# A fused attention and mixer kernel: first attention with less weight conversion, first products beside the conversion, and a written order of instructions on TensorE

## The chip, the cores and the metric

The kernel runs on one core of one Trainium2 chip. The metric is the device time of one execution in microseconds (us), given as the median of several runs. A profiled run also has a span, from the first to the last instruction; it is 1.7 to 1.9 us shorter than the time of the same run.

## The reference

Four batches, eight heads, 768 positions, head width 48. A gated linear attention comes first; its output is a batch's x of 768 x 384, and a mixer with a low-rank step over the positions and two products with 384 x 1536 weights follows.

```python
f = 1.0 / (1.0 + np.exp(-f_logit))
for t in range(S):
    state = f[:, :, t, :, None] * state + np.einsum('bhd,bhe->bhde', k[:, :, t], v[:, :, t])
    y[:, :, t] = np.einsum('bhd,bhde->bhe', q[:, :, t], state)
# x = y as (B, S, H*D)
h = x.transpose(0, 2, 1) @ U @ V
u = x + h.transpose(0, 2, 1)
out = u + np.maximum(u @ w_ch1, 0.0) @ w_ch2
```

q, k, v, f_logit are float32. The four weights arrive as float64, and the kernel has to convert them itself.

## The kernel before

A **unit** is two heads of one batch: 16 units, four to a batch. A unit's attention goes through ten pieces: gates (transpose f on TensorE, sigmoid), kept keys (transposes of kT, copy to kb), keep (the scan X on VectorE), keys (kT), states (products ds, the scan st), scores (products sc, masked into A), read-back (the scan Y), read-out (products y from st), queries (qT) and inner products (y from A). The mixer has a low rank (ph), mixing (pu and an addition), a turn (put), 18 **first products** (pz, evicted to z by ScalarE with the Relu) and six **second products** (po) for batch 0; later batches use seven half-size products per pair (pw). The products of one batch are written between the attention pieces of the next as **fill**.

Each 64-bit weight slab costs two ScalarE, three VectorE and one GpSimd instruction:

```python
nc.scalar.activation(f, hi.bitcast(F32), AF.Abs)
nc.scalar.activation(r, lo, AF.Copy, scale=2.0**-29)
nc.vector.tensor_scalar(f, f, SMALLEST, LARGEST, ALU.max, ALU.min)
nc.vector.tensor_scalar(y, y, 3, 0x3FFFFFFF, ALU.logical_shift_left, ALU.bitwise_and)
nc.vector.scalar_tensor_tensor(y, hi, 0xC0000000, y, ALU.bitwise_and, ALU.bitwise_or)
nc.gpsimd.tensor_tensor(flat.bitcast(I32), y.bitcast(I32), r, ALU.add)
```

The second product of batch 0, one accumulation group of 12 matmuls (24 instructions in the trace):

```python
def ch2(a, s):
    t = 2 * a + s
    pm = ps_mm.tile([P, 512], F32, name="po", tag="mm")
    for i in range(NFC):
        nc.tensor.matmul(pm[:, 0:DM], lhsT=z[a, i // NI][:, i % NI, s * P : (s + 1) * P],
                         rhs=w2[:, i, :], start=(i == 0), stop=(i == NFC - 1))
    o = three.tile([P, DM], F32, name="o")
    nc.vector.tensor_tensor(o, x[:, t, :], pm[:, 0:DM], ALU.add)
    store(t, o)
```

The main loop (cut). A scheduler decides each engine's order; the recorded order is its hint.

```python
early = first - 7                     # eight weight slabs as fill of batch 0's attention
todo = [(1, f) for f in loads[:early]]
...
for b in range(B):
    fill = Fill(todo, HP * 10)
    for n in range(b * HP, (b + 1) * HP):
        kept, states, scores, read, inner = attend(n)
        gates, keep, keys, read_back, queries = prepare(n + 1)
        for piece in [gates, kept, keep, keys, states, scores, read_back, read, queries, inner]:
            fill()
            piece()
    fill.rest()
    m = mixer(b)
    if b == 0:
        start = NFC // 2 + NFC // 4   # nine first products beside the conversion
        for i, (_, piece) in enumerate(m.before + m.main[0:start]):
            if loads and (i % 2 == 0 or i >= len(m.before)):
                loads.pop(0)()
            piece()
        ...
        todo = m.main[start:]         # nine first and four second products fill batch 1
```

## Time and profile before

| | before |
|---|---|
| time, median | 575.3 us (575.49 in the runs beside the changed kernel) |
| TensorE busy, of the span of 573.6 us | 518.0 us, 90% |
| mean granted TensorE clock | 0.970 of full |

The table of stretches of the kernel before follows: start and end in us, length, then busy us and number of instructions of TensorE (PE), its weight loads, VectorE (DVE), ScalarE (ACT) and GpSimd (POOL), and the granted clock, the transfer engines' share and GB/s.

```profile
core 0: us, PE busy (x) PEld busy (x) DVE busy (x) ACT busy (x) POOL busy (x), PEclk, DMA share, GB/s
...
27.50:69.90 42.40, 28.22 (x659) 24.77 (x660) 36.07 (x49) 17.37 (x38) 6.98 (x7) 0.76 1.04 197
...
124.20:230.30 106.10, 97.63 (x998) 68.71 (x996) 54.90 (x57) 23.29 (x49) 7.25 (x4) 0.97 0.39 97
230.30:573.60 343.30, 328.94 (x3055) 290.35 (x3053) 143.96 (x190) 67.99 (x131) 22.79 (x12) 0.99 0.13 35
```

Read the length against PE busy: what is missing is idle time. In the rest of batch 0's attention (first row) TensorE works 28.2 of 42.4 us at a clock of 0.76, VectorE 36.1. In batch 1's attention (second row) TensorE is idle for 8.5 us, 8.4 of them in one wait of ds for kb, and the clock is nearly full. The last row, batches 2 and 3 and the end, has little left to win.

### The profile page before, as it was taken

To read this page: it belongs to the slowest core of one execution; us is meant where nothing else is said; L and a number is where in the kernel's file an instruction comes from. 1 tells how busy PE (TensorE), PEld (TensorE's weight loads), DVE (VectorE), ACT (ScalarE), POOL (GpSimd) and SP (SyncE) were. 2 spreads that over 40 slices of the span, in tenths; PEclk is the share of its full clock that TensorE was granted. 3 is DMA by queue.
4 is the path that set the end of the run, shared out by engine and by line. 5 is a ranking of instruction groups with operands and counts; after the bars stand their busy time and mean duration, and the time that the engine had idled before them with its cause. 6 is when DMAs were issued, how large, how long until landed. Compare 5 with 4: busy or idle time off the path is not lost.

```text
span 573.6 us, 12007 instructions
## 1 busy us (share of the span) xinstructions
PE 518.0 (90%) x5277; PEld 430.7 (75%) x5277; DVE 294.8 (51%) x390; ACT 146.0 (25%) x293; POOL 61.0 (11%) x63
## 2 busy tenths in 40 slices
PE   5676699799997699998999979998999999999996
PEld 4565568558864565888889867888889977898996
DVE  4788777964357753185766553186343141212132
ACT  3344356512221311222222112222121102201110
POOL 3011113420002110020211200020200000000000
PEclk9887799999999799999999989999999999999999
DMA  9599734716233525131533220010000000000000
GB/s 161 128 232 196 160 108 147 211 28 136 65 85 74 137 53 137 24 103 43 139 75 92 80 62 29 1 22 1 29 2 3 29 1 30 1 0 29 0 29 33
DMA packets 75307, 41.76 MB, mean 73 GB/s; under 512 B 65774, under 2 KB 68846, under 8 KB 75246
## 3 DMA queue, kind: packets, MB, share of 16 engines
q1 hardware_dynamic: 75246, 40.91, 30.6%
q8 instruction: 43, 0.70, 0.5%
q14 instruction: 18, 0.15, 0.1%
HBM read 36.18 MB, written 4.72 MB: 71 GB/s over the span
## 4 chain that ended last, share of the span: by engine, by line
PE 71%; DVE 18%; DMA 3%; ACT 3%; issue 2%; SPq 1%; POOL 1%; DVEq 0%; POOLq 0%; ACTq 0%
PE pz L157 26%; PE pw L194 22%; PE po L171 6%; PE y L590 3%; DVE X L465 3%; DMA f_raw<-in_f_logit_dram 3%; PE pt L433 3%; DVE w_y L62 3%; PE y L572 3%; PE pu L138 2%; PE ds L543 2%; DVE Y L482 2%; DVE fT L414 2%; PE sc L513 2%; PE put L147 2%
## 5 line engine op out<-in xcount | busy, mean ns | idle before, releaser
L157 PE MATMUL pz<-uT,w 128*128 128x256 f32 x864 | 196.4, 384 | 2.9 <-ACT z L162 2.3
L157 PEld LDWEIGHTS pz<-uT,w 128*128 128x128 f32 x864 | 162.2, 191 | 27.5 <-ACT z L162 3.7
L194 PE MATMUL pw<-w,w_raw 128*128 128x192 f32 x432 | 76.6, 333 | 4.1 <-DVE o L210 4.1
L162 ACT ACTIVATE z<-pz 128x512 f32<-128x512 f32 x72 | 42.7, 595 | 135.1 <-PE pz L157 131.0
L194 PEld LDWEIGHTS pw<-w,w_raw 128*128 128x128 f32 x432 | 71.7, 193 | 5.6 <-DVE o L210 4.9
L194 PE MATMUL pw<-w,z 128*128 128x192 f32 x324 | 56.5, 329 | 3.8 <-ACT z L162 3.8
L194 PEld LDWEIGHTS pw<-w,z 128*128 128x128 f32 x324 | 52.7, 190 | 5.5 <-ACT z L162 4.1
L171 PE MATMUL po<-w,z 128*128 128x384 f32 x144 | 48.7, 492 | 2.8 <-ACT z L162 1.8
L171 PEld LDWEIGHTS po<-w,z 128*128 128x128 f32 x144 | 26.6, 190 | 22.0 <-issue 2.8
L557 DVE TENSOR_TENSOR_SCAN st<-added,whole 128x576 f32<-128x576 f32 x16 | 21.6, 1352 | 37.3 <-ACT added L549 37.3
L465 DVE TENSOR_TENSOR_SCAN X<-fz,ends 128x768 f32<-128x768 f32 x16 | 29.8, 1863 | 21.1 <-ACT fz L454 13.6
L448 POOL TENSOR_TENSOR kT<-kT,X 128x768 f32<-128x768 f32 x8 | 14.6, 1821 | 238.2 <-DVE kT L414 179.9
L185 DVE TENSOR_TENSOR w_raw<-z 128x768 f32<-128x768 f32 x9 | 8.8, 978 | 56.6 <-ACT z L162 56.6
L572 PE MATMUL y<-st,qT 48*64 48x48 f32 x704 | 20.5, 268 | 14.0 <-DVE st L557 14.0
L590 PEld LDWEIGHTS y<-v_nat,A 64*64 64x64 f32 x768 | 26.4, 148 | 7.1 <-ACT seen L579 3.3
L64 POOL TENSOR_TENSOR w<-w_y,w_r 128x384 int32<-128x384 int32 x24 | 23.9, 995 | 66.8 <-DVE w_y L63 66.8
L590 PE MATMUL y<-v_nat,A 64*64 64x48 f32 x768 | 28.4, 232 | 2.8 <-ACT seen L579 2.8
L572 PEld LDWEIGHTS y<-st,qT 48*64 48x64 f32 x704 | 17.6, 157 | 17.4 <-issue 16.2
L482 DVE TENSOR_TENSOR_SCAN Y<-fz,starts 128x768 f32<-128x768 f32 x16 | 29.4, 1838 | 0.5
L543 PEld LDWEIGHTS ds<-v_nat,kb 64*64 64x64 f32 x768 | 15.6, 145 | 16.9 <-ACT kb L535 11.3
L543 PE MATMUL ds<-v_nat,kb 64*64 64x48 f32 x768 | 19.4, 233 | 9.1 <-ACT kb L535 9.0
L414 DVE STREAM_TRANSPOSE fT<-f_raw 128x768 f32<-128x768 f32 x8 | 16.7, 2086 | 9.9 <-POOL qT L448 7.9
(87 smaller groups left out, 491.2 us busy)
## 6 DMA issues: line engine op xcount, KB each, us to landing
w_raw<-in_moe_w_ch_dram SPq DMA_DIRECT2D x24, 384.0 KB, 3.7
v_nat<-in_v_dram SPq DMA_DIRECT2D x32, 144.0 KB, 3.5
out_dram<-o SPq DMA_DIRECT2D x24, 192.0 KB, 2.2
f_raw<-in_f_logit_dram SPq DMA_DIRECT2D x31, 142.0 KB, 3.6
k_raw<-in_k_dram SPq DMA_DIRECT2D x31, 142.0 KB, 2.9
q_raw<-in_q_dram SPq DMA_DIRECT2D x31, 142.0 KB, 3.8
f_raw<-in_f_logit_dram SPq DMA_DIRECT2D x16, 144.0 KB, 5.4
k_raw<-in_k_dram SPq DMA_DIRECT2D x16, 144.0 KB, 4.5
```

Of the source, the lines that this page charges most:

```text
L64: nc.gpsimd.tensor_tensor(flat.bitcast(I32), y.bitcast(I32), r, ALU.add)
L157: nc.tensor.matmul(pm[:, i * 2 * P : (i + 1) * 2 * P], lhsT=w1[:, m, o : o + P], rhs=uT[a][:, m, :], start=(m == 0), stop=(m == NDC - 1))
L162: nc.scalar.activation(z[a, c][:, k : k + 2, :].rearrange("p i t -> p (i t)"), pm, AF.Relu)
L171: nc.tensor.matmul(pm[:, 0:DM], lhsT=z[a, i // NI][:, i % NI, s * P : (s + 1) * P], rhs=w2[:, i, :], start=(i == 0), stop=(i == NFC - 1))
L194: nc.tensor.matmul(pm[:, n * HM : (n + 1) * HM], lhsT=lhs[:, i, :], rhs=rhs[:, i, :], start=(i == 0), stop=(i == NI - 1))
L414: nc.vector.transpose(t.rearrange("p (i c) -> p c i", c=TB), bass.AP(src_tile.tensor, src_tile.offset, [list(src_tile.ap[0]), [D, TB], [1, ...
L465: nc.vector.tensor_tensor_scan(backwards(X, S - 1, S), backwards(f, S, S), backwards(ends, S - 1, S), 0.0, ALU.mult, ALU.add,)
L482: nc.vector.tensor_tensor_scan(Y, f[:, 0:S], starts, 0.0, ALU.mult, ALU.add)
L543: nc.tensor.matmul(ds[par * PAD : (par + 1) * PAD, s, c * D : (c + 1) * D], lhsT=T["kb"][part[s], par, c, :], rhs=vt[part[s], c, par, :], ...
L557: nc.vector.tensor_tensor_scan(st, added[:, 0 : D * NCH], whole.rearrange("p e c -> p (e c)"), 0.0, ALU.add, ALU.mult)
L572: nc.tensor.matmul(o(c % 2, par, c // 2), lhsT=T["q"][rows[par], chunk[c]], rhs=T["st"][rows[par], c, :], start=(c <= 2), stop=False, skip ...
L590: nc.tensor.matmul(o(s, par, c), lhsT=T["A"][part[s], par, c, :], rhs=vt[part[s], c, par, :], start=False, stop=True, skip_group_check=True,)
```

## The change

Its intent: TensorE should not idle through the start. Batch 0's attention keeps only three weight slabs. All 18 first products of batch 0 run beside the rest of the conversion, so that only its six second products are left for batch 1. TensorE's order is the written one for the whole program, VectorE's up to batch 1. The operands of batches 2 and 3 are loaded in rows of 32 and 16 elements instead of rows that overlap. The change has further parts: the mixer's additions get a high priority in the scheduler's order, w1 is converted in slabs of 128 columns that reach over all three of its chunks, some buffers are no longer shared, and in batches 2 and 3 the kept keys come before the gates. The diff, cut to its core:

```diff
+        def add(*args):
+            with tc.high_priority(offset=AHEAD):
+                nc.vector.tensor_tensor(*args)
...
-            nc.vector.tensor_tensor(o, x[:, t, :], pm[:, 0:DM], ALU.add)
+            add(o, x[:, t, :], pm[:, 0:DM], ALU.add)
...
+        self.firsts = [p for j in range(NI) for a in range(NA) for p in [first(a)[j]]]
+        self.seconds = [p for a in range(NA) for p in second(a)]
...
-                    nc.sync.dma_start(
-                        out=dst[p0 : p0 + rows, :],
-                        in_=bass.AP(head.tensor, head.offset + part * NB, [[TB * D, rows], [1, W]]),
-                    )
+                    nc.sync.dma_start(
+                        out=raw[n % 2][nm][p0 : p0 + NB, :].rearrange("p (c d) -> p c d", d=NB)[:, :, 0:n_ch],
+                        in_=head[:, :, part * NB : part * NB + n_ch],
+                    )
...
+    ctx.enter_context(tc.manual_schedule(engines={nc.tensor.engine}))
+    with tc.manual_schedule(engines={nc.vector.engine}):
+        ready = {n: prepare(n) for n in range(2)}
+        for piece in ready[0] + ready[1][:1]:
+            piece()
+        for n in range(HP):
+            kept, states, scores, read, inner = attend(n)
+            _, keep, keys, read_back, queries = ready.pop(n + 1, [lambda: None] * 5)
+            if n + 2 < HP:
+                ready[n + 2] = prepare(n + 2)
+            gates = ready[n + 2][0] if n + 2 < HP else lambda: None
+            for piece in [kept, keep, keys, states, scores, read_back, gates, read, queries, inner]:
+                piece()
+            if n and loads:
+                loads.pop(0)()
+        m = mixer(0)
+        for i, (_, piece) in enumerate(m.before + m.firsts):
+            if loads and (i % 3 == 0 or i >= len(m.before)):
+                loads.pop(0)()
+            piece()
+        for f in loads:
+            f()
+        todo, after = m.seconds[:4], m.seconds[4:]
+        for i, piece in enumerate(prepare(HP)):
+            piece()
+            if i == 0:
+                todo.pop(0)[1]()
+        attention(1, todo)
+        m = start_mixer(1, after)
```

More of the change, by code (lines that the diff above doesn't have):

```diff
@@ L21 @@
 PAD = 64
+AHEAD = 1000
 LEAST = 1e-18
@@ L42, in load, with shaped @@
         rows, n = dst.shape[0], dst.free_size()
-        flat = dst if len(dst.shape) == 2 else dst.rearrange("p c n -> p (c n)")
         T = {}
+        def shaped(t):
+            return t if len(dst.shape) == 2 else t.rearrange("p (c n) -> p c n", c=dst.shape[1])
         def start():
             raw = T["raw"] = pool.tile([P, WP], U64, name="w_raw", bufs=RAW)[0:rows, 0:n]
-            if len(dst.shape) == 3:
-                raw = raw.rearrange("p (c n) -> p c n", c=dst.shape[1])
-            dma.dma_start(out=raw, in_=w)
+            dma.dma_start(out=shaped(raw), in_=w)
         def end():
@@ L63, in end @@
             nc.vector.scalar_tensor_tensor(y, hi, 0xC0000000, y, ALU.bitwise_and, ALU.bitwise_or)
-            nc.gpsimd.tensor_tensor(flat.bitcast(I32), y.bitcast(I32), r, ALU.add)
+            nc.gpsimd.tensor_tensor(dst.bitcast(I32), shaped(y.bitcast(I32)), shaped(r), ALU.add)
         return start, end
@@ L109, with __init__ @@
 class Mixer:
-    def __init__(self, nc, b, x, U, V, w1, w2, sums, ident, out, two, three, zp, ps_mm):
+    def __init__(self, tc, b, x, U, V, w1, w2, sums, ident, out, two, three, zp, ps_mm, wide=False):
+        nc = tc.nc
         P = nc.NUM_PARTITIONS
@@ L138, in mix @@
             nc.tensor.matmul(pm[:, 0:DM], lhsT=V[:, t * P : (t + 1) * P], rhs=h[0], start=True, stop=True)
-            nc.vector.tensor_tensor(x[:, t, :], x[:, t, :], pm[:, 0:DM], ALU.add)
+            add(x[:, t, :], x[:, t, :], pm[:, 0:DM], ALU.add)
         def turn(t):
@@ L160, in ch1 @@
             if k == 0:
-                z[a, c] = zp.tile([P, NI, 2 * P], F32, name="z")
+                own = wide and 2 * a + c >= 3
+                z[a, c] = zp.tile([P, NI, 2 * P], F32, name="zw" if own else "z")
             nc.scalar.activation(z[a, c][:, k : k + 2, :].rearrange("p i t -> p (i t)"), pm, AF.Relu)
@@ L183, in sums_of @@
                 S[i] = s.bitcast(F32).rearrange("p (i t) -> p i t", t=P)
-            add = nc.vector.tensor_tensor
             add(S[1], part(a, 1, 0), part(a, 1, 1), ALU.add)
@@ L202, in seven @@
             x0, x1 = x[:, 2 * a, :], x[:, 2 * a + 1, :]
-            add = nc.vector.tensor_tensor
             if step == 0:
@@ L260, in quarters, with place @@
     q = {(i, j): w2[:, i * NI : (i + 1) * NI, j * HM : (j + 1) * HM] for i in range(2) for j in range(2)}
-    sums = {i: pool.tile([P, NI, HM], F32, name=f"w2_{i}") for i in range(1, 4)}
-    sums[4] = q[0, 1]
+    sums = {4: q[0, 1]}
     sub = nc.vector.tensor_tensor
+    def place():
+        for i in range(1, 4):
+            t = pool.tile([P, NI, 2 * P], F32, name="zw")
+            sums[i] = t.rearrange("p i t -> p (i t)")[:, 0 : NI * HM].rearrange("p (i d) -> p i d", d=HM)
     return sums, [
+        place,
         lambda: sub(sums[1], q[0, 1], q[0, 0], ALU.subtract),
@@ L293, in factored_path @@
     TB = S // NB
-    W = (TB - 1) * D + NB
+    W = TB * NB
     G = NCH // 2
     TURNED = 2
-    assert S % (2 * P) == 0 and H % 2 == 0 and NB < D <= PAD and PAD == 2 * NB and S % NB == 0
+    assert S % (2 * P) == 0 and H % 2 == 0 and NB < D <= PAD and PAD == 2 * NB and S % NB == 0 and W == NBL * 2 * PAD
     assert DM % P == 0 and FF % P == 0 and FF % WP == 0 and DM == WP and DM <= 512 and R % 32 == 0 and P % R == 0 and P // R <= NBL and NFC % 4 == 0
@@ L314, in factored_path @@
     nat = [
-        {nm: t[:, 0 : NBL * 2 * PAD].rearrange("p (c h d) -> p c h d", h=2, d=PAD) for nm, t in slot.items()}
+        {nm: t.rearrange("p (c h d) -> p c h d", h=2, d=PAD) for nm, t in slot.items()}
         for slot in raw
@@ L334, in load_unit @@
                 continue
-            dst = raw[n % 2][nm]
             for par in range(2):
-                head = src[nm][b, 2 * hp + par]
+                head = src[nm][b, 2 * hp + par].rearrange("(i c) d -> i c d", c=TB)
                 for part in range(2):
                     p0 = par * PAD + part * NB
-                    last = n == NU - 1 and par == 1 and part == 1
-                    rows = NB - 1 if last else NB
+                    n_ch = min(NB, D - part * NB)
                     nc.sync.dma_start(
-                        out=dst[p0 : p0 + rows, :],
-                        in_=bass.AP(head.tensor, head.offset + part * NB, [[TB * D, rows], [1, W]]),
-                    )
-                    if last:
-                        w = W - (2 * NB - D)
-                        nc.sync.dma_start(
-                            out=dst[p0 + rows : p0 + NB, 0:w],
-                            in_=bass.AP(head.tensor, head.offset + part * NB + rows * TB * D,
-                                        [[TB * D, 1], [1, w]]),
-                        )
+                        out=raw[n % 2][nm][p0 : p0 + NB, :].rearrange("p (c d) -> p c d", d=NB)[:, :, 0:n_ch],
+                        in_=head[:, :, part * NB : part * NB + n_ch],
+                    )
         v_tiles[n] = three.tile([P, NBL, 2, D], F32, name="v_nat")
@@ L397, in factored_path @@
     weights += [load(V[:, o : o + WP], copies(moe_V, P // R, o, WP)) for o in range(0, S, WP)]
-    weights += [
-        load(w1[:, c, o : o + WP], moe_w_ch1[c * P : (c + 1) * P, o : o + WP])
-        for o in range(0, FF, WP)
-        for c in range(NDC)
-    ]
-    first = len(weights)
-    sums, to_sum = quarters(nc, const, w2)
+    w1_rows = moe_w_ch1.rearrange("(c p) f -> p c f", p=P)
+    weights += [load(w1[:, :, o : o + P], w1_rows[:, :, o : o + P]) for o in range(0, FF, P)]
+    sums, to_sum = quarters(nc, zp, w2)
     weights += [load(w2[:, i, :], moe_w_ch2[i * P : (i + 1) * P, :]) for i in range(NFC)]
@@ L415, in turned @@
             t.rearrange("p (i c) -> p c i", c=TB),
-            bass.AP(src_tile.tensor, src_tile.offset, [list(src_tile.ap[0]), [D, TB], [1, NB]]),
+            src_tile.rearrange("p (c d) -> p c d", d=NB),
         )
@@ L456, in gates @@
                 return
-            fT = one.tile([P, S], F32, name="fT", tag="Y")
+            fT = one.tile([P, S], F32, name="fT")
             turned(fT, r["f"])
@@ L480, in read @@
         def read():
-            Y = T["Y"] = one.tile([P, S], F32, name="Y", tag="Y")
+            Y = T["Y"] = one.tile([P, S], F32, name="Y")
             nc.vector.tensor_tensor_scan(Y, f[:, 0:S], starts, 0.0, ALU.mult, ALU.add)
@@ L493, in mixer @@
     def mixer(b):
-        return Mixer(nc, b, x_tiles[b], U, V, w1, w2, sums if b else None, ident, out, two, three, zp, ps_mm)
+        return Mixer(tc, b, x_tiles[b], U, V, w1, w2, sums if b else None, ident, out, two, three, zp, ps_mm, b == 0)
     def attend(n):
@@ L605, in factored_path, with attention @@
     loads = ahead_by(RAW - 1, weights)
-    early = first - 7
-    todo = [(1, f) for f in loads[:early]]
-    loads = loads[early:]
-    for piece in prepare(0):
-        piece()
-    after = []
-    for b in range(B):
+    def attention(b, todo):
         fill = Fill(todo, HP * 10)
@@ L619, in factored_path @@
                 order = [gates, kept, keep, keys, states, scores, read_back, read, queries, inner]
+                if (n + 1) // HP >= TURNED:
+                    order[0:2] = [kept, gates]
             else:
@@ L625, in factored_path, with start_mixer @@
         fill.rest()
+    def start_mixer(b, after):
         m = mixer(b)
-        if b == 0:
-            start = NFC // 2 + NFC // 4
-            for i, (_, piece) in enumerate(m.before + m.main[0:start]):
-                if loads and (i % 2 == 0 or i >= len(m.before)):
-                    loads.pop(0)()
-                piece()
-            for f in loads:
-                f()
-            todo = m.main[start:]
-            for i, f in enumerate(to_sum[:3]):
-                todo.insert(len(todo) - 4 + 2 * i, (1, f))
-        else:
-            after[1:1] = m.before[0:1]
-            after[3:3] = m.before[1 : 1 + NBL]
-            after += m.before[1 + NBL :]
-            if b == 1:
-                after.append((1, to_sum[3]))
-            for _, piece in after:
-                piece()
-            todo = m.main
@@ L648, in factored_path @@
-        after = m.after
+        pieces = after[:1] + m.before[:1] + after[1:2] + m.before[1 : 1 + NBL] + after[2:] + m.before[1 + NBL :]
+        for _, piece in pieces:
+            piece()
+        return m
+    ctx.enter_context(tc.manual_schedule(engines={nc.tensor.engine}))
[10 more added lines that the diff above has]
+            for piece in [kept, keep, keys, states, scores, read_back, gates, read, queries, inner]:
+                piece()
+            if n and loads:
[14 more added lines that the diff above has]
+        m = start_mixer(1, after)
+        for f in to_sum:
+            f()
@@ L650, in factored_path @@
+    for b in range(2, B):
+        todo, after = m.main, m.after
+        attention(b, todo)
+        m = start_mixer(b, after)
+    todo, after = m.main, m.after
     low = one.tile([P, 1], F32, name="low")
@@ L907, in mixer @@
     def mixer(b):
-        return Mixer(nc, b, x_tiles[b], U, V, w1, w2, None, ident, out, two, three, zp, ps_mm)
+        return Mixer(tc, b, x_tiles[b], U, V, w1, w2, None, ident, out, two, three, zp, ps_mm)
     FILLS = NL + 3
```

## The prediction

> **What bounds the kernel now.** I began with the busy rows in 40 slices of 14.3 us (tenths; the clock row is the granted TensorE clock).
>
> ```profile
> PE   5676699799997699998999979998999999999996
> DVE  4788777964357753185766553186343141212132
> PEclk9887799999999799999999989999999999999999
> ```
>
> The run has two regimes. Up to about slice 8 (124 us) TensorE is at 5 to 7 tenths, on a clock of 7 to 8 tenths in slices 1 to 4, and VectorE is the fuller engine. Later TensorE is nearly full. Next I read the chain that ended last, in order of time (start, duration, what).
>
> ```profile
> 15.15 12.29 DMA f_raw<-in_f_logit_dram
> 27.57 1.53 PE pt L433 x6
> ...
> 43.42 2.32 DVE X L465
> 46.03 0.87 DVE kT L445
> 47.07 1.76 DVE Y L482
> 48.82 1.26 DVE st L557
> 50.22 1.52 PE y L572 x44
> 51.74 1.47 PE pt L433 x6
> 53.21 2.19 PE y L590 x48
> 55.40 0.82 PE pt L433 x6
> ...
> 94.12 1.06 DVE w_y L62
> 96.07 1.06 DVE w_y L62
> ```
>
> Three things limit the start: a load for unit 2 that lands only at 27.5 us; a serial chain of 13.6 us per attention unit (42.59 to 56.24 from one gate to the next), with slow matmuls (1.47 us for six transposes that take 0.82 us warm); and the weight conversion, one slab per 1.95 us from 92 to 120 us. The costs come from the groups by form (busy us, mean ns):
>
> ```profile
> L157 PE MATMUL pz<-uT,w 128*128 128x256 f32 x864 | 196.4, 384 | 2.9 <-ACT z L162 2.3 <-ACT uT L149 0.4 <-POOL w L64 0.2
> L62 DVE TENSOR_SCALAR w_y<-w_y 128x384 uint32<-128x384 uint32 x26 | 21.1, 810 | 0.8
> L63 DVE SCALAR_TENSOR_TENSOR w_y<-w_raw,w_y 128x384 uint32<-128x384 uint32 x26 | 15.1, 582 | 0.7
> L64 POOL TENSOR_TENSOR w<-w_y,w_r 128x384 int32<-128x384 int32 x24 | 23.9, 995 | 66.8 <-DVE w_y L63 66.8
> ```
>
> Finally the waits of TensorE from 124 us to the end: what is left to win there.
>
> ```profile
> PE ds L543 <- ACT kb L535: 8.4, 1, 8.4
> PE pw L194 <- DVE o L210: 4.1, 1, 4.1
> PE pw L194 <- ACT z L162: 3.8, 2, 1.9
> ```
>
> **What the Trainium skill says.** "SBUF — State Buffer", section "SBUF: two separate sides", calls the port pair of VectorE and GpSimd an exclusive lock. The trace agrees: the shift (L62) takes 0.35 us alone and 1.05 us when a GpSimd add (0.99 us) runs; 0.35 + 1.05 + 0.55 is the 1.95 us. "TensorE: Matmul & The Clock Gate", Part 1, has a cold clock of half speed, released after some 3.4 us of activity; the 1.47 against 0.82 us above agrees. "PSUM — Partial Sum Buffer", "Engine vs sequencer instructions", says the ScalarE and VectorE queues are strict FIFO and matmuls keep their order; so the static orders of the changed program decide who waits behind whom. "DMA: Bandwidth & Descriptors", "Specifications", puts line rate at 512 B or more; here the 192-byte-row loads still moved 1.18 MB in about 7 us per unit when the queue was full.
>
> **The change part by part.** TensorE's arithmetic is unchanged, so I follow two clocks, where TensorE is free and where the in-order VectorE is.
>
> (1) Attention of batch 0. Conversion drops from eight slabs to three (U and two of V), and the next gates are issued one unit ahead. But unit 2's load stands in the same place of the same load queue, behind the V loads, so it again lands at 27.5 us; and now its transposes stand ahead of unit 0's read-out in TensorE's written order, so unit 0 waits too. From there: transposes to 29.1, read-out 1.2, query transposes 1.5, inner products 2.2, and unit 0 ends at 33.5 instead of 25.7. After that VectorE sets the pace: X 1.76 + small 0.56 + kT 0.95 + st 1.35 + A 0.95 + Y 1.76 + qT 0.95 = 8.3 us per unit, plus a slab. Scan X of unit 2 starts at 32.6, that of unit 3 at 41.9, unit 3's queries end at 50.2, V slab to 52, then kept keys, ds, st, read-out, inner, copy (0.8 + 0.9 + 0.65 + 1.3 + 1.2 + 2.2 + 0.6): low rank starts at **60 us, before 69.9**. Gain 10 us.
>
> (2) Low rank, mix, turn. On VectorE the x additions stand between slabs, so mixing waits: additions at 63.6 (2), one slab, 66.7 (3), one slab, 70.2 (1). First products start at **74.5, before 84**; the stage takes 14.5 us for 9.3 us of TensorE work (1.4 + 4.85 + 3.0).
>
> (3) All 18 first products, 12 matmul instructions each, 2.59 us apiece (23.58 us for 108): 46.6 us if TensorE were free. But ScalarE's compiled order puts two slabs (2 x 1.95 = 3.9 us) between one eviction and the next for the first nine. Slab 5 of w1/w2 ends about 76.7 on VectorE; the first eviction is at 78.8, the ninth at 78.8 + 8 x 3.9 = 110; with two PSUM buffers eight products are left: **done at 110.5 + 8 x 2.6 = 131.3**. The conversion ends near 112 (before 120.4), so this is 8 us earlier, but 10 us of TensorE time lie idle beside it, before 5.
>
> (4) Batch 1 attention. Before, nine first products and four second ones filled it; now only the six second ones (7.94 us each) remain, and VectorE follows the written order. Unit 4's X scan stands behind the addition of the first second product: 131.3 + 0.8 + 7.9 + 0.6 = 140.7. I followed the chain unit by unit. TensorE idles about 4 us in unit 4 (kT, then qT), 2.5 in unit 5, 2.5 in unit 6 (each waits for st), 4.6 in unit 7 (st stands behind an addition, kT and fT, 2.1 us each), and 3 in the mixing (a transpose and a scan stand between the x additions): 17 us. TensorE work: six times 7.94 = 47.6, attention 30, low rank to turn 9.3, together 87. So batch 1's first products begin at 131.3 + 87 + 17 = 235. In the kernel before they begin at 230.3, with 1.4 us of unit 8 already done: **behind by 6 us**. The gain of (1) is spent.
>
> (5) Batches 2 and 3. TensorE's sequence hardly differs. The 8.4 us wait (kb behind the gate of unit 8) lay before 230 and is gone, counted in (4). Of the 8 us of waits after 231, high-priority additions should take 4 to 5. The loads without double reading move a third less but in rows of 128 and 64 bytes: 12 x 768 + 1536 rows per unit. At the measured 0.8 us per 768-row load of a full queue that is, as an estimate, 11 us per unit against 23 us of unit time: hidden. The transpose is still 2.08 us.
>
> Sum: 573.6 + 6 - 5 = 574.6 us of span; the time is 1.7 us more (575.3 against 573.6): 576.3. I take **574**, since the hand chain takes each handover at its worst.
>
> **The rivals.** *The intended gain arrives:* conversion hides under first products at one slab per 2.6 us, attention 0 runs at 8.5 us per unit from 13 us on. It would end near 131 - 20 and give 550 to 558. For it: VectorE needs only 1.95 us of each 2.6 us. Against it: the 27.5 us landing and the two-slab order on ScalarE, both fixed by the build. *VectorE's written order becomes the bound in batch 1* more strongly than I count, with TensorE cold after each gap (0.6 us per group): 583 to 587. For it: the 1.47 us groups above. *The small-row loads become the wait* in batches 2 and 3: if such a row cost twice a 192-byte one, 22 us per unit would touch the 23 us available, and 5 to 10 us would be added. Against it: the load share there is 0 to 3 tenths.
>
> **Range and chances.** The chain up to 131 us I hold good to 4 us, batch 1 to 5, the rest to 4: together about 8 us, a little wider towards faster, where the first rival lies: **561 to 585**. Faster by over 2% means under 563.8 us: 0.15. Slower means over 586.8 us: 0.06. Within 2%: 0.79.
>
> **What would show it.** Step 1: TensorE's first wait still ends with unit 2's f load at 27 to 28 us; ph starts near 60. Step 2: pz starts near 74 to 75. Step 3: the first nine z are 3.9 us apart, the last pz ends near 131. Step 4: waits of y on st and of pt on kT or qT between 132 and 235, in sum some 14 us, and the batch 1 pz start at 233 to 238. Step 5: no DMA among TensorE's or VectorE's waits after 240. The prediction is wrong if f of unit 2 lands early, if evictions come every 2.6 us, or if batch 1's fill covers the chain; then the time falls below 563.

## The result, and the profile after

The changed kernel takes **593.85 us** (592.15 to 596.04, four runs) against 575.49 us (575.16 to 577.47): ratio **1.031**, interval 1.027 to 1.036. It is slower, and outside the predicted range. Executions over 1.5% slower than the fastest of the same kernel are left out of the means. A ratio is the mean time of one kernel's fast runs over that of the other's fast runs of the same rounds, so not quite the ratio of the medians quoted. The profiled run of the changed kernel, from which all its lines and stretches below come, is the slowest of the four (596.04 us). The changed kernel was not run again beside the later experiments, so differences from it of about 1% rest on ratios from different rounds.

The busy rows and the clock row of the changed kernel, in slices of 14.9 us, tenths:

```profile
PE   5396886799889869799979997999999999999996
DVE  4466399910762675749647576047531151122132
PEclk9786599999798678999999999999999999999998
```

The clock row has two troughs (slices counted from 0): slices 1 to 4, attention of batch 0, deeper than before; and a new one in slices 10 to 15, 149 to 238 us, attention of batch 1, where the row of before has nines and a single seven. The stretches, in the columns of the table above:

```profile
28.50:67.80 39.30, 31.50 (x734) 28.14 (x735) 24.07 (x33) 12.44 (x27) 4.88 (x4) 0.67 0.86 151
67.80:82.70 14.90, 12.46 (x42) 5.59 (x42) 8.28 (x17) 6.33 (x15) 2.92 (x3) 0.73 0.35 98
82.70:140.30 57.60, 48.77 (x217) 40.46 (x218) 36.59 (x59) 28.34 (x56) 20.00 (x21) 1.00 0.41 117
140.30:252.20 111.90, 97.59 (x1060) 65.66 (x1058) 64.71 (x71) 22.84 (x50) 8.42 (x4) 0.86 0.45 70
252.20:594.20 342.00, 327.15 (x3089) 288.58 (x3089) 146.62 (x194) 69.29 (x132) 22.80 (x12) 1.00 0.14 27
```

The fourth row is the finding: the stretch of batch 1's attention holds 15.4 us less of the mixer's products of batch 0 than before (six second products of 7.94 us instead of 5 x 7.94 + 9 x 2.59) and some 4 us more of the attention, since before part of unit 4 lay ahead of the stretch. Yet TensorE is busy just as long, 97.6 us, at a clock of 0.86, and is idle for 14.3 us instead of 8.5. It ends 22 us later than in the kernel before. How this looks in TensorE's order of time (start, length, what, in brackets the idle time just before it and what ended it; batch 0 first, then the first products, then batch 1):

```profile
28.55 1.51 PE L436 MATMUL pt<-ident,f_raw 128*128 128x128 f32 x6 [10.39 <-DMA f_raw<-in_f_logit_dram]
...
64.19 2.80 PE L593 MATMUL y<-v_nat,A 64*64 64x48 f32 x48 [0.25 <-ACT seen L582]
67.82 2.77 PE L135 MATMUL ph<-x,U 128*32 128x384 f32 x12 [0.83 <-ACT x L599]
...
91.80 2.83 PE L166 MATMUL pz<-uT,w 128*128 128x256 f32 x12 [1.05 <-ACT z L173]
96.04 2.86 PE L166 MATMUL pz<-uT,w 128*128 128x256 f32 x12 [1.42 <-ACT zw L173]
```

```profile
152.51 0.58 PE L534 MATMUL pt<-ident,kT 64*128 64x64 f32 x12 [1.71 <-DVE kT L448]
...
156.72 10.16 PE L182 MATMUL po<-w,z 128*128 128x384 f32 x24
...
168.78 1.60 PE L593 MATMUL y<-v_nat,A 64*64 64x48 f32 x48
...
173.58 0.89 PE L516 MATMUL sc<-qT,kT 48*64 48x64 f32 x48
176.59 1.23 PE L575 MATMUL y<-st,qT 48*64 48x48 f32 x44 [2.12 <-DVE st L560]
177.75 1.20 PE L436 MATMUL pt<-ident,q_raw 128*128 128x128 f32 x6
178.88 2.80 PE L593 MATMUL y<-v_nat,A 64*64 64x48 f32 x48
...
217.71 1.52 PE L575 MATMUL y<-st,qT 48*64 48x48 f32 x44 [4.37 <-DVE st L560]
219.48 2.80 PE L593 MATMUL y<-v_nat,A 64*64 64x48 f32 x48 [0.25 <-ACT seen L582]
222.20 9.85 PE L182 MATMUL po<-w,zw 128*128 128x384 f32 x24
```

The same 48 inner products take 1.60 us in one unit and 2.80 us in the next; the slow ones come after a wait for st. A whole second product, 7.9 us at full clock, takes 10.2 and 9.9 us. In the kernel before, first products stood between sc and y:

```profile
142.42 0.89 PE L513 MATMUL sc<-qT,kT 48*64 48x64 f32 x48
143.25 2.86 PE L157 MATMUL pz<-uT,w 128*128 128x256 f32 x12
146.03 1.24 PE L572 MATMUL y<-st,qT 48*64 48x48 f32 x44
```

The waits of TensorE and of VectorE in the changed kernel from 140 to 253 us (in total, times, longest):

```profile
PE y L575 <- DVE st L560: 8.6, 3, 4.4
```

```profile
DVE o L143 <- PE po L182: 60.4, 6, 28.2
```

Each engine waits for the other. VectorE stands before the addition of a second product until its 24th instruction is done (28.2 us of the 60.4 lie before the first of them, the other five waits come to 32.2), and what is written behind the addition, scans among it, is late; then TensorE stands before the read-out.

### The profile page after: what moved, and what is told of

Same layout as the page of the kernel before. It is cut to its first block, busy times and chain, and to the rows that moved or that the text cites. A ratio compares the mean times of both kernels' runs of the same rounds, so it can differ in the third digit from the quotient of the medians.

```text
span 594.2 us, 11997 instructions
## 1 busy us (share of the span) xinstructions
PE 528.4 (89%) x5277; PEld 437.3 (74%) x5277; DVE 293.8 (49%) x390; ACT 147.2 (25%) x293; POOL 63.5 (11%) x63
## 4 chain that ended last, share of the span: by engine, by line
PE 71%; DVE 18%; DMA 3%; ACT 3%; issue 2%; POOL 2%; SPq 1%; DVEq 0%; POOLq 0%; ACTq 0%
PE pz L166 26%; PE pw L204 19%; PE po L182 9%; PE y L593 5%; DVE w_y L65 3%; DMA f_raw<-in_f_logit_dram 3%; PE y L575 3%; PE pt L436 2%; DVE w_y L66 2%; PE ds L546 2%; DVE st L560 2%; PE pu L147 1%; DVE X L468 1%; DVE fT L417 1%; DVE w_y L64 1%
## 5 line engine op out<-in xcount | busy, mean ns | idle before, releaser
L173 ACT ACTIVATE z<-pz 128x512 f32<-128x512 f32 x63 | 37.5, 595 | 117.6 <-PE pz L166 113.4
L204 PE MATMUL pw<-zw,w_raw 128*128 128x192 f32 x324 | 56.2, 328 | 2.2 <-DVE o L143 2.2
L204 PEld LDWEIGHTS pw<-zw,w_raw 128*128 128x128 f32 x324 | 52.8, 190 | 3.7 <-DVE o L143 3.5
L143 DVE TENSOR_TENSOR w_raw<-z 128x768 f32<-128x768 f32 x18 | 20.4, 1132 | 57.3 <-ACT z L173 57.2
L593 PEld LDWEIGHTS y<-v_nat,A 64*64 64x64 f32 x768 | 30.3, 166 | 7.2 <-ACT seen L582 4.8
L593 PE MATMUL y<-v_nat,A 64*64 64x48 f32 x768 | 32.4, 250 | 3.0 <-ACT seen L582 3.0
L143 DVE TENSOR_TENSOR o<-x,po 128x384 f32<-128x384 f32 x6 | 3.3, 555 | 60.4 <-PE po L182 60.4
L575 PEld LDWEIGHTS y<-st,qT 48*64 48x64 f32 x704 | 18.4, 169 | 15.4 <-issue 12.1
L182 PE MATMUL po<-w,z 128*128 128x384 f32 x72 | 28.0, 549 | 0.0
L182 PE MATMUL po<-w,zw 128*128 128x384 f32 x72 | 25.9, 517 | 0.0
L147 PE MATMUL pu<-h,V 128*128 128x384 f32 x48 | 21.1, 561 | 4.3 <-DVE x L143 3.0
L65 DVE TENSOR_SCALAR w_y<-w_y 128x384 uint32<-128x384 uint32 (+1 forms) x27 | 24.2, 895 | 0.9
```

Source lines behind the costliest of these rows:

```text
L147: nc.tensor.matmul(pm[:, 0:DM], lhsT=V[:, t * P : (t + 1) * P], rhs=h[0], start=True, stop=True)
L173: nc.scalar.activation(z[a, c][:, k : k + 2, :].rearrange("p i t -> p (i t)"), pm, AF.Relu)
L204: nc.tensor.matmul(pm[:, n * HM : (n + 1) * HM], lhsT=lhs[:, i, :], rhs=rhs[:, i, :], start=(i == 0), stop=(i == NI - 1))
L575: nc.tensor.matmul(o(c % 2, par, c // 2), lhsT=T["q"][rows[par], chunk[c]], rhs=T["st"][rows[par], c, :], start=(c <= 2), stop=False, skip ...
L593: nc.tensor.matmul(o(s, par, c), lhsT=T["A"][part[s], par, c, :], rhs=vt[part[s], c, par, :], start=False, stop=True, skip_group_check=True,)
```

## The experiments

All ratios are to the kernel before, run in the same rounds. The suspects were the row loads; the first weight loads, which stand ahead of unit 2's operands; the move of nine first products out of batch 1; the written orders; and the low clock. Later runs asked by what means the written order costs.

| run | time us | ratio | low rank starts | last first product of batch 0 ends | first products of batch 1 start |
|---|---|---|---|---|---|
| before | 575.5 | 1 | 69.9 | 202.6 | 230.3 |
| after | 593.9 | 1.031 | 67.8 | 140.4 | 252.2 |
| e2 | 589.8 | 1.022 | 62.9 | 134.2 | 246.0 |
| e12 | 588.3 | 1.021 | 64.9 | 136.1 | 244.9 |
| e4a | 575.5 | 0.996 | 68.3 | 136.4 | 238.9 |
| e4b | 586.2 | 1.018 | 64.7 | 136.8 | 245.2 |
| e7 | 568.0 | 0.988 | 58.7 | 127.1 | 225.0 |
| e13 | 576.3 | 0.998 | 65.1 | 137.7 | 229.6 |
| e16 | 574.5 | 0.996 | 65.0 | 137.6 | 229.3 |
| e17 | 589.7 | 1.023 | 66.9 | 139.5 | 244.3 |
| e15 | 569.3 | 0.985 | 60.7 | 132.0 | 223.9 |
| e18 | 557.3 | 0.966 | 59.1 | 129.4 | 218.6 |

The last three columns come from the profiled run of each. Five of the runs (e3, e10, e13, e16, e17) have the changed kernel's code up to the low rank, and start it between 64.8 and 67.2 us, the changed kernel itself at 67.8: differences of up to 3 us in that column show nothing by themselves.

### e1_rows_only: the row loads alone, in the kernel before

```diff
-    W = (TB - 1) * D + NB
+    W = TB * NB
-    in_=bass.AP(head.tensor, head.offset + part * NB, [[TB * D, rows], [1, W]])
+    in_=head[:, :, part * NB : part * NB + n_ch]
```

> The kernel before with one part of the change alone: the operands of batches 2 and 3 in rows of 128 and 64 bytes, without double reading. Theory A (the loss lies in batch 1, whose attention has lost its fill of first products, so that TensorE waits on VectorE's chain and cools): the time stays within 0.5% of the kernel before, 573 to 578 us, and no DMA wait of over 3 us in all appears on TensorE or VectorE after 240 us. Theory C (the small rows cost the 18 us): 585 us or more.

Measured: 576.58 us, ratio 1.001 (0.995 to 1.007). The rows of 128 and 64 bytes cost nothing that can be seen, and gain nothing. They are not the cause. No wait for a load shows on TensorE or VectorE after 240 us.

### e2_weights_later: the first weight loads behind unit 2's operands

```diff
-    loads = ahead_by(RAW - 1, weights)
     def attention(b, todo):
...
         for piece in ready[0] + ready[1][:1]:
             piece()
+        loads = ahead_by(RAW - 1, weights)
```

> The changed kernel, with the first three weight loads (U and two of V) issued behind unit 2's operands instead of ahead of them. If the first attention gained little because unit 2's load stood behind the V loads (its transposes started at 28.5 us): those transposes now start at 19 to 22 us, the low rank product at 60 to 63 us instead of 67.8, and the time is 586 to 590 us. If that landing is hidden anyway, the time stays at 592 to 596.

Measured: 589.84 us, ratio 1.022 (1.017 to 1.028). Unit 2's gates start at 18.6 us instead of 28.5; then unit 3's wait 8.2 us at 35 us, behind the same weight loads. Low rank begins 4.9 us earlier than in the profiled run of the changed kernel, 1.9 us before the earliest run with its code, and the median is 4.0 us lower. The landing is at most a part, not the whole.

### e3_nine_left: nine first products beside the conversion, nine left for batch 1

```diff
-        for i, (_, piece) in enumerate(m.before + m.firsts):
+        for i, (_, piece) in enumerate(m.before + m.main[:9]):
...
-        todo, after = m.seconds[:4], m.seconds[4:]
+        todo, after = m.main[9:], m.after
```

Two slabs go to each of the nine.

> The changed kernel, with only nine first products beside the conversion and the other nine left as fill for batch 1's attention, as in the kernel before; written orders and loads stay. Theory A: the conversion still ends at 116 to 120 us, batch 1's attention starts some 20 us earlier, its first products begin at 230 to 238 us instead of 252, TensorE's clock there is 0.95 or more, and the time is 572 to 581 us. Theory B (the written order on TensorE is the cost): 588 us or more.

Measured: 584.68 us, ratio 1.014 (1.009 to 1.019), between what the two theories expected. Batch 1's first products start at 232.7 us, as in the kernel before, and from 160 to that point the clock is 0.95: with nine pieces of 2.6 us in the fill the trough is gone. But the rest then takes 347.4 us instead of 342.0, and some 8 us of the 18 lost stay lost. In that rest stands a wait of 4.2 us of batch 1's second products (pw) for z, which the changed kernel does not have, and the 24 matmuls behind it take 5.67 us, where a like group later takes 4.17.

### e4a_sched_pe and e4b_sched_both: the written orders taken away

For e4a only TensorE's:

```diff
-    ctx.enter_context(tc.manual_schedule(engines={nc.tensor.engine}))
     with tc.manual_schedule(engines={nc.vector.engine}):
```

> The changed kernel, with TensorE's order left to the scheduler again; VectorE's written order in batches 0 and 1 stays. Theory B (the written order on TensorE is the cost): 580 us or less. Theory A: 587 to 598 us, since VectorE's chain and the missing fill of batch 1 are as before.

Measured: 575.53 us (573.53 to 580.50), ratio 0.996 (0.991 to 1.002). One line gives back 18 us. The profiled run was the slowest of the four. In its TensorE timeline, second products go into a wait in parts:

```profile
149.00 0.81 PE L182 MATMUL po<-w,z 128*128 128x384 f32 x2
150.47 0.92 PE L546 MATMUL ds<-v_nat,kb 64*64 64x48 f32 x48 [0.66 <-issue]
```

The scheduler placed 2 of 24 instructions of po ahead of ds. It still left 7.3 us of waits of y on st in batch 1. For e4b VectorE's written order was removed as well:

```diff
-    with tc.manual_schedule(engines={nc.vector.engine}):
+    if True:
```

> The changed kernel with both engines' orders left to the scheduler. If VectorE's written order (the X scan of unit 4 behind an addition of a second product) costs by itself, this is below the run with the scheduler on TensorE alone (575.5): 565 to 572. If it only matters together with TensorE's written order: 573 to 579. If it is a gain: 580 or more.

Measured: 586.15 us, ratio 1.018 (1.014 to 1.022), with 10.6 us of waits of y on st. So VectorE's written order is worth some 2% where the scheduler orders TensorE; TensorE's written order, as it stands, costs 3.5%.

### e6_sched_nine: TensorE by the scheduler, with nine first products left for batch 1

The edits of e3 and e4a together.

> The changed kernel with TensorE's order left to the scheduler and nine first products left as fill for batch 1, so the two single edits together. If the written order and the lost fill are separate losses, the gains add: ratio to the kernel before 0.996 - 0.017 = 0.979, 560 to 567 us. If they are one loss seen twice (the scheduler's order already covers the chain that has no fill), nothing is added: 572 to 578 us.

Measured: 579.77 us, ratio 1.007 (1.003 to 1.012). The two remedies do not add: batch 1's first products start at 229.9 us, but the rest takes 347.8 us. The wait of 4.2 us for z stands in this rest too; why it comes was not tested.

### e7_sched_late and e8_sched_nine_late: weights later, by the scheduler

e7 is e4a with the first weight loads behind unit 3's operands:

```diff
-            if n and loads:
+            if n == 0:
+                loads = ahead_by(RAW - 1, weights)
+            else:
                 loads.pop(0)()
```

> TensorE's order left to the scheduler, and the first three weight loads issued only behind unit 3's operands. If the landing of unit 2 and 3 is worth what the earlier run of that kind showed (0.9%), 568 to 572 us, with both units' gate transposes waiting under 3 us for their loads. If the conversion, which starts later, takes it back: 574 to 580 us.

Measured: 567.97 us (566.50 to 571.01), ratio 0.988 (0.983 to 0.993). Low rank starts at 58.7 us, batch 1's first products at 225.0. This is faster than both kernels. e8 adds e3's edit:

> All three edits together. If the three losses are separate: ratio 0.970, 555 to 561 us, and it beats both kernels. If they overlap: 566 to 575 us.

Measured: 570.80 us, ratio 0.993 (0.988 to 0.997). Again nine products left over gain nothing in the end.

### e9_warm and e10_warm_b1: useless matmuls ahead of each read-out

48 matmuls of sc's kind, written ahead of the read-out into a tile that it overwrites; in e9 for batches 0 and 1, in e10 for batch 1 alone.

```diff
+            if b < 2:                      # e10: if b == 1
+                for i in range(2):
+                    for c in range(NBL): ...
+                                nc.tensor.matmul(y[part[s], par, 0:C], lhsT=T["k"][...], rhs=T["q"][...],
+                                    start=True, stop=True, skip_group_check=True)
```

> The changed kernel with 48 useless matmuls of 64x64 (96 instructions, some 1.7 us warm) ahead of the read-out of each of the eight units of batches 0 and 1, into the tile that the read-out then clears: the work stands where TensorE waits for the state scan. If half of the loss in the written order is the cold clock after such waits (the inner products take 2.8 us there instead of 1.6), the granted clock rises to 0.96 or more and the time falls by 5 to 12 us, to 582 to 589. If the waits alone are the loss and the clock is a bystander, the added work costs 0 to 8 us: 594 to 602.

Measured: 599.83 us, ratio 1.042 (1.038 to 1.046): slower, since in batch 0 the added work lies on the path (low rank at 74.9 us). By the time alone this is the range expected for the clock as a bystander; the reading by stretches was made afterwards. In batch 1: 1443 instructions instead of 1060, yet TensorE's busy time falls from 97.6 to 95.4 us, at a clock of 0.95 instead of 0.86, and the stretch from 111.9 to 105.2 us. More work takes less time there, at a higher clock.

> The changed kernel with the useless matmuls of the warm run in batch 1 alone (four units), where the stretch from the end of the first products of batch 0 to the first products of batch 1 was 105 us with them and 112 us without. If the cold clock is a part of the loss there: that stretch is 104 to 107 us again and the time 586 to 590 us. If the warm run's gain there was given back behind it (its later stages were 3 us longer), 591 to 596.

Measured: 590.36 us (588.01 to 595.64), ratio 1.026 (1.022 to 1.029): some 0.6% less than the changed kernel, but the intervals of the two ratios overlap. The profiled run was the slowest of five; its stretch of 110.0 us, at a clock of 0.91, missed the expected 104 to 107. So this run agrees with the clock as a part, but neither shows nor sizes it.

### e11_before_late: the later weight loads in the kernel before

```diff
     load_unit(1)
+    for piece in prepare(0):
+        piece()
     loads = ahead_by(RAW - 1, weights)
```

> The kernel before with the first weight loads behind unit 2's operands, nothing else. If the landing of unit 2 stands on its chain as the chain shows (12.3 us of load at 15 to 27.6 us), the low rank product starts 4 to 7 us earlier and the time is 568 to 572. If VectorE's conversion, which starts later, takes it back, 574 to 578.

Measured: 574.03 us, ratio 0.996 (0.992 to 1.000). Unit 2's gates start at 23.4 us instead of 27.6, and low rank at 68.7 instead of 69.9. By the interval the landing is worth 0 to 4 us there; what takes the rest was not shown.

### e12_gates_last: the gates of unit n + 2 after the inner products of unit n

```diff
-            for piece in [kept, keep, keys, states, scores, read_back, gates, read, queries, inner]:
+            for piece in [kept, keep, keys, states, scores, read_back, read, queries, inner, gates]:
```

> The changed kernel with one piece moved in the written order of batch 0's attention: the gate transposes of unit n+2 come after unit n's inner products instead of before its read-out. If unit 0's read-out waiting behind unit 2's load is what spoils the first attention: unit 0's inner products end near 26 us instead of 35, scan X of unit 2 starts at 31 instead of 33.9, and the low rank product at 64 to 66 instead of 67.8 us; time 589 to 592. If it is the load itself, no change: 592 to 596.

Measured: 588.33 us, ratio 1.021 (1.017 to 1.025). Unit 0's inner products now run at 24.5 us instead of 32.9: unit 0 did wait for the load of unit 2 without need. The ratio is 1% lower than that of the changed kernel. Low rank starts at 64.9 us, but so does e3 without this edit (64.8), so it is not shown that the 1% was won there.

### e13_split: the written order kept, the second products divided

Each second product of the fill becomes six pieces of two matmuls, written between the attention pieces; the first one, which had stood whole behind unit 4's gates, is spread over its first three pieces.

```diff
-            for i in range(NFC):
-                nc.tensor.matmul(...)
-            o = three.tile([P, DM], F32, name="o")
+            def some(k):
+                if k == 0:
+                    T["pm"] = ps_mm.tile([P, 512], F32, name="po", tag="mm")
+                for i in range(2 * k, 2 * k + 2):
+                    nc.tensor.matmul(T["pm"][:, 0:DM], ...)
+                if k == NFC // 2 - 1:
+                    o = three.tile([P, DM], F32, name="o") ...
+            return [(4 * DM, lambda k=k: some(k)) for k in range(NFC // 2)]
...
-            if i == 0:
+            for _ in range(2 if i < 3 else 0):
                 todo.pop(0)[1]()
```

> The changed kernel, written order on TensorE kept, but each second product of batch 0 that fills batch 1's attention (24 matmuls, 7.9 us warm and 9.6 to 10.2 us there) is cut into six pieces of two or more matmuls that are written between the attention's own products; the addition of X of the first unit no longer stands behind one of them. Theory A (a written order costs time because undivided 8 to 10 us blocks cannot sit in waits of 2 to 4 us, so the waits stay idle and TensorE's clock falls in them): batch 1's stretch shrinks from 111.9 us to 100 to 104 us, the run takes 580 to 586 us. Theory B (the stretch is set by the chain of VectorE and ScalarE, or by the clock whatever fills the waits): 591 to 597 us.

Measured: **576.25 us** (574.78 to 576.95), ratio 0.998 (0.994 to 1.002), more than Theory A had expected. The stretch of batch 1 in the table of stretches, and TensorE's timeline in one unit:

```profile
137.60:229.60 92.00, 86.62 (x1059) 55.74 (x1057) 63.33 (x71) 22.88 (x50) 8.02 (x4) 1.00 0.52 85
```

```profile
167.68 0.89 PE L524 MATMUL sc<-qT,kT 48*64 48x64 f32 x48
168.51 1.56 PE L187 MATMUL po<-w,z 128*128 128x384 f32 x4
170.16 1.24 PE L583 MATMUL y<-st,qT 48*64 48x48 f32 x44
171.33 1.56 PE L187 MATMUL po<-w,z 128*128 128x384 f32 x4
172.73 0.82 PE L444 MATMUL pt<-ident,q_raw 128*128 128x128 f32 x6
173.47 1.60 PE L601 MATMUL y<-v_nat,A 64*64 64x48 f32 x48
```

Where the changed kernel waited 2.12 us between sc and y, a piece of 1.56 us stands now, no wait shows, and the inner products behind take 1.60 us instead of 2.80. The waits of y on st in this stretch fall from 8.6 to 0.2 us. The same work (1059 instructions) takes 86.6 us at full clock instead of 97.6 at 0.86, and idle time falls from 14.3 to 5.4 us. The sum is the 19.9 us by which the stretch is shorter. (The profiled runs are the slowest of the changed kernel and the fastest of e13; the medians differ by 17.6 us.) The order is still written by hand, so nearly all of the 18 us were the cost of writing blocks of 8 us.

The division does two things that no run parts. Pieces stand in TensorE's waits: in the unit shown st ends at 170.02 us, 1.45 us after sc, so the piece did fill a wait that was still there. And VectorE, whose written order has the addition behind the last piece, stands less long before the additions, from 140 to 253 us:

```profile
DVE o L143 <- PE po L187: 12.4, 3, 6.1
```

In the changed kernel five waits came to 32.2 us, the first one left out.

### e16_split_rest and e17_first_moved: which half of e13's edit

e16 keeps the division for three of the four fill products and leaves the first whole in its old place. e17 has all whole and moves only the first:

```diff
-            if i == 0:
+            if i == 2:
                 todo.pop(0)[1]()
```

> The divided version (576.3 us, ratio 0.998) changed two things at once: the second products in the fill were cut, and the addition of the first one no longer stood ahead of unit 4's scan X. Here only the cutting is kept for three of the four fill products; the first second product is undivided and in its old place. If the cutting is what counts: 577 to 582 us (it loses some 3 us: the 1.7 us wait of the transposes on kT and the late first scan). If the place of the first one counts as much: 584 to 590 us.

> The changed kernel with undivided second products; only the first of them is written after unit 4's kept keys instead of after its gates, so that unit 4's scan X and kT no longer stand behind its addition. If the cutting is what counts: 589 to 594 us, the changed kernel but for 2 or 3 us. If the first one's place counts as much as the cutting: 583 to 587 us.

Measured: e16 574.54 us, ratio 0.996 (0.992 to 1.001); e17 589.66 us, ratio 1.023 (1.019 to 1.026). The division does it alone, and e16 came out faster than either expectation. The move is worth 0.9% where the products are whole, and nothing where they are divided.

### e14_sched_late_gl, e15_written_late_gl_split and e18_sched_late_split: the remedies combined

e14 is e7 with e12's edit. e15 has the written order with e7's weight loads, e12's gates and e13's division. e18 is e7 with e13's division.

> TensorE's order by the scheduler, the first weight loads behind the operands of unit 3 (the fastest version so far, 568 us), and in batch 0 the gates of unit n+2 recorded after the inner products of unit n, not before. If where the gates are recorded still matters with a scheduler (it follows recorded order among ready work): low rank starts 2 to 4 us earlier and the run takes 563 to 567 us. If the scheduler passes the waiting gates by itself: 566 to 571 us, the same.

Measured: 572.03 us, ratio 0.990 (0.984 to 0.995), level with e7. Under the scheduler no effect of the gates' place is seen.

> TensorE's order written by hand again, with three mendings at once: the first weight loads behind the operands of unit 3, the gates of unit n+2 after the inner products of unit n in batch 0, second products cut into six pieces in batch 1. Theory A (the 18 us that the written order costs are these placements): 565 to 573 us, level with the scheduler's 568 us. Theory B (something else in a written order costs, such as the lost choice at every single wait): 578 us or more.

Measured: 569.27 us (566.09 to 570.34), ratio 0.985 (0.980 to 0.990), level with e7. A written order with the three mended places is as good as the scheduler's with whole products.

> TensorE by the scheduler, first weight loads behind unit 3's operands, second products recorded in six pieces in batch 1. If a scheduler divides the second products well enough by itself: level with the undivided version of the same kind (568 us, ratio 0.988), so 566 to 570 us. If it still leaves waits that recorded pieces would fill (it left 7.3 us of waits for the state scan in batch 1 in an earlier run): 560 to 565 us, the fastest of all.

Measured: **557.28 us** (556.91 to 558.42), ratio 0.966 (0.962 to 0.970). This is the fastest version, 3.4% under the kernel before and some 6% under the changed one. Its rows:

```profile
PE   4857987789999998999899989999999999999996
...
PEclk9897899999999999999999999999999999999999
```

From slice 5 on the clock row has nines only. In batch 1 the waits of y on st are 0.2 us, where e7's had 7.3. Batch 1's first products start 11.7 us earlier than before, and the rest takes 337.2 instead of 343.3 us; the two make up the span's 17.8 us. So the scheduler also needs small pieces: it had moved whole products into waits only in part. The written order is not free either: e15, with the same division and weight loads (and e12's gates, which did nothing in e14), is 12 us slower than e18, 6.4 us of it behind batch 1's attention (343.6 against 337.2 us). What it lacks there was not tested.

## Why the prediction was wrong

The prediction put the changed kernel level with the one before; it is 3.1% slower. Its chain of reasons held in kind, and two of its terms were sized wrongly: in step 4 the work was counted as if TensorE ran at full clock, in step 1 partly so. By stages, the span of 594.2 us against the 574.6 us that the prediction summed up:

| step | predicted us | measured us | miss |
|---|---|---|---|
| 1, low rank starts | 60 | 67.8 | +7.8 |
| 2, from there to the first products | 14.5 | 14.9 | +0.4 |
| 3, first products | 56.8 | 57.7 | +0.9 |
| 4, batch 1's attention | 103.7 | 111.7 | +8.0 |
| 5, the rest | 339.6 | 342.0 | +2.4 |

**Step 1 failed in size.** The late load did land at 28 us and unit 0 did wait for it; e12 confirms that this wait was not needed. From there the chain was followed with VectorE's pace and matmuls between the warm and the slow durations. The measured clock was 0.67. (The other five runs with this code start low rank at 64.8 to 67.2 us, so the miss is 4.8 to 7.8 us.) The scan X of unit 3 starts at 44.3 instead of 41.9 us. In that unit the conversion's GpSimd addition for U took 1.89 us beside that scan (the larger V slabs took 0.99 to 1.00), ScalarE came to kb late, and ds waited 2.85 us for it; VectorE's queries end at 55.1 instead of 50.2 us. The last stretch from the V slab to low rank was put at 8.0 us and took 11.5, with ds at 1.53 instead of 0.9 us, the read-out at 1.52 instead of 1.2, the inner products at 2.80 instead of 2.2.

**Steps 2 and 3 held.** The first products start 14.9 us after low rank, the evictions were about 4 us apart (91.80 to 96.04 is 4.24, the next ones 3.9), and the stage took 57.7 us. The rival in which the evictions come every 2.6 us did not arrive.

**Step 4 failed in its work term.** The idle time was put at 17 us and is 14.3, for the reasons named there: kT, st behind the additions. But "TensorE work: ... together 87" assumed full clock throughout; the trace has 97.6. The divided version shows that the 87 itself was counted well: with the waits filled the same instructions take 86.6 us. So beside the idle time itself, which was foreseen, the work stretched by 11.0 us, which was not. The rival that named it, a cold TensorE after each gap with 583 to 587 us, was the right mechanism and was given too little: 0.6 us per group was taken from small transposes, but a whole second product lost 2.2 us, and three of the four sets of inner products 1.2 each.

**Step 5** promised 5 us; the rest is 1.3 us shorter than before, and 1.4 us of unit 8 had to be made up, so the gain was about 2.7. The two waits of pw named there fell from 7.9 us to 2.2, but waits that the kernel before does not have came to 5.5 us (y for a copy 2.5, pz for an addition 1.6, pu for an addition 1.4). No load is among TensorE's waits of note there, as predicted.

What also went wrong is a step that the prediction did not take: it listed where six 7.94 us products stand, and did not ask whether the same waits could hold anything else. e13 shows that they could. Two slips of the recorded text carry nothing: unit 0's parts in step 1 sum to 34.0 us, not 33.5, and slices 5, 6 and 8 of its first busy row stand at 9 tenths, not at 5 to 7.

**What stays open.** Where the waits go, the low clock goes too (e13, e16, e15, e18: clock 1.00 in batch 1's attention), but it does not follow their length alone. e4a and e7 have the same waits of y on st there, 7.3 us, and were granted 0.90 and 0.95, which makes stretches of 102.5 and 97.9 us; e17 has the changed kernel's 8.6 us of them and 0.92 instead of 0.86. e9 and e10, with useless work in the waits, got 0.95 and 0.91 from the same code in that stretch. So the 11.0 us are the size in one profiled run, and how the granted clock follows short waits is not settled. How much of the gain of dividing comes from filled waits, and how much from additions that block VectorE less, stays open. In batch 0's attention the clock stayed low even in the divided version (0.77 from 27 to 65 us), and no run filled the waits there with useful work.

## What to carry to other kernels

Work that is meant to fill waits must be cut to the size of the waits, whoever orders it: here 2 to 4 us of wait, pieces of 1.5 us, and 18 us gained by dividing alone. When counting a stage with idle gaps, cost its work at the clock that gaps of this kind left in the trace, not at the warm duration. Before a scheduler's choice is fixed by hand, look at what it now puts into each wait, because a written order must carry all of that itself.

## What the Trainium skill lacked or had wrong

- "TensorE: Matmul & The Clock Gate", Part 1, has in its table of states that the clock falls after at least one idle window of about 3.4 us, and gives no length for the shorter idle times that the part also mentions. Here inner products took 2.80 us instead of 1.60 behind a wait of 2.12 us between short matmuls, and in one stretch of 112 us the low clock cost 11.0 us, 1.9% of the run.
- "DMA: Bandwidth & Descriptors", "Specifications", gives 512 B as the least size for line rate. It is silent on loads that lie hidden: rows of 128 and 64 bytes in two batches changed the time by a factor of 1.001 (0.995 to 1.007).
- I found no page that tells how large pieces of filling work should be against the waits that they fill: 7.9 us blocks against 1.5 us pieces made 594 into 576 us with a written order, and 568 into 557 us with the scheduler's.
